# Queries and keys by crossbar transfer from the ninth step on in an attention and mixer kernel

## The chip, the cores and the metric

The kernel runs on one core of a Trainium2 chip. The metric is the device time of one execution in microseconds; the kernel before took 371.93 us (median of 3 runs, 371.04 to 372.26). A core has five engines with instruction streams of their own: TensorE (PE, with its weight loads as PEld), VectorE (DVE), ScalarE (ACT), GpSimd (POOL) and SyncE (SP). In this kernel GpSimd issues the loads from memory, and SyncE issues the transposing transfers and nearly all of the output stores.

## The reference

Attention with squared ReLU over 8 batches of 12 heads, 448 tokens and 64 dimensions, and then a mixer with a token part and a channel part:

```python
scores = scale * np.matmul(q, k.transpose(0, 1, 3, 2))       # 8 x 12 heads, 448 x 448
attn = np.maximum(scores, 0.0) ** 2 / S
attn_out = np.matmul(attn, v)                                # 448 x 64 per head
x = attn_out.transpose(0, 2, 1, 3).reshape(B, S, H * D)      # 8 x 448 x 768

xt = x.transpose(0, 2, 1)
h = np.maximum(xt @ w_tok1, 0.0) @ w_tok2                    # token part, 448 -> 256 -> 448
u = x + h.transpose(0, 2, 1)
h2 = np.maximum(u @ w_ch1, 0.0) @ w_ch2                      # channel part, 768 -> 1536 -> 768
return (u + h2)
```

## The kernel before

The work goes in 24 steps of four heads each (ND = 24, three steps to a batch, DB = 3). Steps are named by their index, so step 8 is the ninth. Inputs are loaded as bf16 with tokens on the partitions, while the scores need the head dimension there: queries and keys have to be transposed for each step. Up to step 11 TensorE does this through PSUM (`transposes`); from step 12 on (`TDMA = 12`) VectorE puts the four heads next to each other in one buffer, `qk_sb`, and one crossbar transfer on SyncE's queue writes the transposed tile (`transposes_dma`).

```python
TDMA = 12

def transposes(i, place="acc", split=False):          # on TensorE, by 64x64 blocks
    sb = attn.tile([128, 2, 2, S], BF16, name="qkT", bufs=3)
    ...                                               # two PSUM tiles, acc0 and acc1
    for w in (0, 1):                                  # queries, keys
        src = raws.pop((i, "qk"[w]))
        for c in range(QC):                           # 7
            for r in range(2):
                for g in range(2):
                    nc.tensor.matmul(parts[r][...], lhsT=src[h, g, c, :],
                                     rhs=ident[h, h], is_transpose=True, ...)
    for r in range(2):
        nc.vector.tensor_copy(sb[:, r]..., parts[r][:, : 2 * S])

def interleave(i):
    t = attn.tile([128, 2, QC, 2, D], BF16, name="qk_sb", bufs=1)
    qk_tiles[i] = t
    for w in range(2):
        nc.vector.tensor_copy(t[:, w].rearrange("n c g d -> n g c d"),
                              raws.pop((i, "qk"[w])))

def transposes_dma(i):
    sb = attn.tile([128, 2, QC, 128], BF16, tag="qkT", name="qkT_x", bufs=3)
    nc.sync.dma_start_transpose(out=sb..., in_=qk_tiles.pop(i)...)
    qkT[i] = sb
```

The attention output `xT` has to be turned back for the token part (`x_back`: on TensorE up to step 7, by crossbar from step 8 on), and so does the residual `uT` for the last sum of the channel part (`u_back`: two crossbar transfers for each step). `hold_back` lets GpSimd write one element into the target of the residual transposes, so that they start only after a chosen event. The loop from step 4 on, cut to the order of its parts:

```python
for i in range(DB + 1, ND + 2):
    scores(i, 0); scores(i, 1)
    values(i - 1, range(QC)); values_out(i - 1)       # writes xT
    scores(i, 2)
    if TDMA <= i + 2 < ND:
        interleave(i + 2)
    ...                                               # fill: units of channel1 or channel2
    x_back(i - 1)
    if i > 2 * DB + 1:
        if i == 2 * DB + 2:                           # step 8
            hold_back(1, x_tiles[i - 1][:1, 0, 0, :1])
        while u_later and u_later[0] < max(i - 1 - (i == 2 * DB + 2), 0):
            u_back(u_later.pop(0))
    if TDMA <= i + 2 < ND:
        transposes_dma(i + 2)
    if i + PRE < ND:                                  # PRE = 3
        if i - 1 >= XDMA:                             # XDMA = 8
            nc.gpsimd.tensor_copy(gate, x_tiles[i - 1][:1, 1, 3, 127:])
        load_four(i + PRE)
    if i == 5:
        load_wc2(1, 2); load_wt1_last()               # the last of the weights
    square()
    ...
    scores(i, 3); scores(i, 4)
    if i + 1 < min(ND, TDMA):
        transposes(i + 1)
    square()
    ...                                               # fill, then token1_main(i - 1)
    token1_rest(i - 1)                                # from step 7 on
    scores(i, 5); scores(i, 6)
    square()
    ...                                               # fill
    token2(i - 1)                                     # its sums write uT
    if (i - 1) % DB == DB - 1:
        channel_work((i - 1) // DB)
    if i == 2 * DB + 1:                               # step 7
        hold_back(0, uT_tiles[1][:1, 0, :1])
        for _ in range(DB):
            u_back(u_later.pop(0))
    square()
    ...                                               # fill
```

A unit of `channel2` is twelve matmuls into one PSUM tile of two (`bank`), which a sum on VectorE empties into `out_sb`, adding the transposed residual `u_sb`; a store on SyncE's queue follows for each finished row tile.

Of the kernel before, what the change touches and what calls it, by code (L numbers as in the profile page):

```python
# [16 lines left out]
def kernel(  # L17
# [19 lines left out]
    ND = B * H // 4  # L37
# [143 lines left out]
            else:  # L181
                nc.vector.tensor_copy(sb[:, :, 0], queries[:, :, :S])

    TDMA = 12
    qk_tiles = {}

    def interleave(i):
# [4 lines that stand above are left out]
            nc.vector.tensor_copy(  # L192
                t[:, w].rearrange("n c g d -> n g c d"), raws.pop((i, "qk"[w]))
            )

    def transposes_dma(i):
        sb = attn.tile([128, 2, QC, 128], BF16, tag="qkT", name="qkT_x", bufs=3)
        nc.sync.dma_start_transpose(
            out=sb.rearrange("n w c t -> n (w c) t"),
            in_=qk_tiles.pop(i).rearrange("n w c g d -> n (w c g d)"),  # L200
        )
        qkT[i] = sb

    def qk_of(i, h, r):
        sb = qkT[i]
        if i < TDMA:
            return sb[h, r, 0, :], [sb[h, r, 1, c * 64 : (c + 1) * 64] for c in range(QC)]
# [3 lines left out]
    def scores(i, c, alone=False):  # L211
        ps = ps_att.tile([128, 2, 512], FP32, tag="att", name="sc_ps")
        for r in range(2):
            for g in range(2):
                h = slice(64 * g, 64 * (g + 1))
                queries, keys = qk_of(i, h, r)
                nc.tensor.matmul(  # L217
                    ps[64 * r : 64 * (r + 1), g, :S],
                    lhsT=keys[c],
                    rhs=queries,  # L220
                    start=True,
                    stop=True,
                    skip_group_check=True,
                )
        at = attn.tile([128, 2, S], BF16, name="at", bufs=11)
        if alone:
            nc.vector.tensor_scalar(
                out=at, in0=ps[:, :, :S], scalar1=0.0, scalar2=None, op0=ALU.max
            )
        else:  # L230
            nc.scalar.activation(at, ps[:, :, :S], AF.Relu)  # L231
        squares.append(at)
        at2[i, c] = at

    def square(keep=0):
        while len(squares) > keep:
            at = squares.pop(0)
            nc.vector.tensor_tensor(out=at, in0=at, in1=at, op=ALU.mult)  # L238

    def values(i, cs):  # L240
        v_raw = raws[i, "v"]
        if i not in accs:
            accs[i] = [ps_acc.tile([128, 512], FP32, tag=f"acc{r}", name="acc_ps") for r in range(2)]
        ps = accs[i]
        for c in cs:
            at = at2.pop((i, c))
            for r in range(2):
                for g in range(2):
                    h = slice(64 * r, 64 * (r + 1))
                    nc.tensor.matmul(  # L250
                        ps[r][64 * g : 64 * (g + 1), :S],
                        lhsT=v_raw[h, g, c, :],
                        rhs=at[h, g, :],
                        start=(c == 0),
                        stop=(c == QC - 1),
                        skip_group_check=True,
                    )

    def values_out(i, split=False):
        b, d = divmod(i, DB)  # L260
        ps = accs.pop(i)
        for r in range(2):
            if split and r == 1:
                nc.scalar.activation(
                    xT[b % 2][:, 2 * d + r, :S], ps[r][:, :S], AF.Copy, scale=float(alpha2)
                )
                continue
            nc.vector.tensor_scalar(  # L268
                out=xT[b % 2][:, 2 * d + r, :S],
                in0=ps[r][:, :S],  # L270
                scalar1=float(alpha2),
                scalar2=None,
                op0=ALU.mult,
            )
        if i > 2 * DB - 1:
            for r in range(2):
                nc.vector.tensor_scalar(
                    out=xT[b % 2][:, 2 * d + r, S:],
                    in0=ps[r][:, S - 64 : S],
                    scalar1=float(alpha2),  # L280
                    scalar2=None,
                    op0=ALU.mult,
                )
# [119 lines left out]
    def chunks(b):  # L403
        half = NT // 2
        return range(half) if b % 2 == 0 else range(half, NT)
# [12 lines left out]
    def hold_back(b, src):  # L418

        u_tiles[b] = mix.tile([128, NP, NT - NT // 2, 128], BF16, name="u_sb", bufs=3)  # L420
        for p in range(NP):
            nc.gpsimd.tensor_copy(u_tiles[b][:1, p, 0, :1], src)

    def channel1(b, e):
        if b % 2 == 0 and e == 0 and b > 0:
            r2_tiles[b // 2] = mix.tile([128, EC, 2 * S], BF16, name="r2_sb")
        uT, r2 = uT_tiles[b // 2], r2_tiles[b // 2]
        off = (b % 2) * S
        ps = ps_mm.tile([128, 512], FP32, tag="bank", name="m1_ps")
        for g in range(CC):  # L430
            nc.tensor.matmul(  # L431
                ps[:, :S],
                lhsT=wc1[:, g, e * 128 : (e + 1) * 128],
                rhs=uT[:, g, off : off + S],
                start=(g == 0),
                stop=(g == CC - 1),
            )
        nc.scalar.activation(r2[:, e, off : off + S], ps[:, :S], AF.Relu)  # L438
# [87 lines left out]
    def channel_work(b):  # L526
        for e in range(2 if b == 0 else 0, EC):
            queue.append((C1, lambda e=e: channel1(b, e)))
        for t in chunks(b):
            for j in range(2):  # L530
                last = b == B - 1 and t == NT - 1 and j == 1
                unit = channel2_last if last else channel2
                args = (b, t) if last else (b, t, j)
                later.append((C2, lambda unit=unit, args=args: unit(*args)))
        if b > 0:
            queue.extend(later)
            later.clear()
# [91 lines left out]
    i = DB  # L629
# [31 lines left out]
    for i in range(DB + 1, ND + 2):  # L661
        slow = i <= 2 * DB
        back = i - 1 < ND
        if i == 2 * DB + 1:
            rate[0] = (EC * C1 + NT * C2) / DB
        if i < ND:
            scores(i, 0)
            scores(i, 1)
        if 0 <= i - 1 < ND:
            values(i - 1, range(QC))  # L670
            values_out(i - 1)
        if i < ND:
            scores(i, 2)
        if TDMA <= i + 2 < ND:
            interleave(i + 2)
        if i - 1 < XDMA:
            fill(1 / 3, least=1)
        if 0 <= i - 1 < ND:
            x_back(i - 1)
        since[0] = 0.0  # L680
        if i > 2 * DB + 1:
            if i == 2 * DB + 2:
                hold_back(1, x_tiles[i - 1][:1, 0, 0, :1])
            while u_later and u_later[0] < max(i - 1 - (i == 2 * DB + 2), 0):
                u_back(u_later.pop(0))
        if TDMA <= i + 2 < ND:
            transposes_dma(i + 2)
        if i + PRE < ND:
            if i - 1 >= XDMA:
# [3 lines that stand above are left out]
            load_wc2(1, 2)  # L693
            load_wt1_last()
        square()
        if i - 1 >= XDMA:
            fill(0.37, least=1)
        if i < ND:
            scores(i, 3)
            scores(i, 4)  # L700
# [3 lines that stand above are left out]
        if slow:  # L704
            token1(i - 1)
            fill(1 / 3, least=1)
        else:
            fill(0.37, least=1, upto=4400 if back else 0)
            if back:
                token1_main(i - 1)  # L710
        if i < ND:
            if not slow:
                token1_rest(i - 1)
            scores(i, 5)
            scores(i, 6)
        elif back:
            token1_rest(i - 1)
        if not slow:
            square()
            fill(0.1, least=1)  # L720
        if back:
            token2(i - 1)
            if (i - 1) % DB == DB - 1:
                channel_work((i - 1) // DB)
        if i == 2 * DB + 1:
            hold_back(0, uT_tiles[1][:1, 0, :1])
            for _ in range(DB):
                u_back(u_later.pop(0))
        square()
        fill(1 / 3 if slow else 0.16, least=1)  # L730
    while queue:
        queue.pop(0)[1]()
# [30 lines left out]
```

## Time and profile before

The profile is of one execution with a span of 369.8 us. A group is a line of the kernel on one engine; its columns are the number of instructions, the time that they were busy, and the mean of one.

| group | count | busy us | mean ns |
|---|---|---|---|
| TensorE, channel1, L431 | 564 | 115.7 | 353 |
| TensorE, channel2, L470 | 660 | 113.2 | 326 |
| TensorE, values, L250 | 672 | 40.7 | 351 |
| TensorE, scores, L217 | 336 + 336 | 27.5 + 25.7 | 360, 356 |
| VectorE, squares, L238 | 168 | 98.1 | 621 |
| VectorE, output sums, L477 | 55 | 30.5 | 555 |
| ScalarE, ReLU of the scores, L231 | 167 | 144.9 | 922 |

| transfers | count | median us to landing |
|---|---|---|
| queries, keys, values, loads from GpSimd | 48, 46, 48 | 4.7, 6.2, 6.5 |
| residual transposes, SyncE | 48 | 2.5 |
| x_back transposes, SyncE | 16 | 3.2 |
| output stores, SyncE | 54 | 3.1 |

TensorE's matmuls overlap in the records, so busy times of its groups can add up to more than the time that passed. "To landing" is the time from the issue on the queue until the transfer's completion was signalled. On the queue SP a row of the timeline gives the time that the queue spent with issuing, not the transfer. The crossbar transfers of queries and keys (12, steps 12 to 23) land 4.0 to 7.9 us after issue, median 6.1.

### The profile page before, as it was taken

The page shows a single profiled execution, that of the slowest core. Times are in us where ns is not written, and L with a number is a line of the kernel's source. Part 1 is how long each engine was busy: PE and PEld are TensorE (multiplying, and loading weights), DVE is VectorE, ACT ScalarE, POOL GpSimd, SP SyncE. Part 2 cuts the span into 40 slices and gives each one's busy share as a digit, 9 for nine tenths or more (in the row PEclk, how much of TensorE's full clock was granted, in tenths as well). Part 3 has the DMA queues.
Part 4 walks back from the last instruction along what each step waited for, and adds up shares of the span by engine and source line. Part 5 has one row for each costly group of instructions (what it writes and reads, how often), then busy time and mean ns, then how long its engine had stood idle before and what let it go on. Part 6 is the DMA issues. An engine that isn't in the chain of part 4 may idle for free.

```text
span 369.8 us, 8951 instructions
## 1 busy us (share of the span) xinstructions
PE 359.9 (97%) x3705; PEld 193.5 (52%) x3705; DVE 207.3 (56%) x414; ACT 210.5 (57%) x313; POOL 98.6 (27%) x185
## 2 busy tenths in 40 slices
PE   8889999999999999999999999999999999999995
PEld 3534555455555644555445545455445555555563
DVE  2986688756575774565654674575564674221031
ACT  4987888777245457735775457753875456402400
POOL 8957347303304404430421404412300000000000
PEclk9999999999999999999999999999999999999999
DMA  8999999932999899969768989759682624233023
GB/s 155 112 193 193 192 206 174 152 48 56 109 189 160 141 236 139 157 118 210 140 109 152 127 185 182 141 99 210 125 144 52 135 57 88 59 71 87 0 74 98
DMA packets 91449, 48.75 MB, mean 132 GB/s; under 512 B 65360, under 2 KB 87952, under 8 KB 91408
## 3 DMA queue, kind: packets, MB, share of 16 engines
q0 software_dynamic: 24496, 21.49, 41.0%
q1 hardware_dynamic: 66528, 26.26, 33.5%
q8 instruction: 29, 0.48, 0.5%
q10 hardware_dynamic: 384, 0.43, 0.4%
q14 instruction: 12, 0.10, 0.1%
HBM read 43.42 MB, written 11.01 MB: 147 GB/s over the span
## 4 chain that ended last, share of the span: by engine, by line
PE 86%; DVE 5%; DMA 4%; POOL 2%; issue 1%; ACT 1%; DVEq 0%; POOLq 0%; ACTq 0%
PE m_ps L431 28%; PE m_ps L470 28%; PE acc_ps L250 9%; PE sc_ps L217 8%; PE h_ps L380 4%; PE t_ps L339 3%; DVE at L238 1%; DMA x_sb<-xT 1%; PE t_ps L321 1%; DVE uT_sb L390 1%; DMA q_raw<-in_q_dram 1%; PE t_ps L355 1%; DMA k_raw<-in_k_dram 1%; PE qkT_ps L140 1%; POOL q_raw L83 1%
## 5 line engine op out<-in xcount | busy, mean ns | idle before, releaser
L231 ACT ACTIVATE at<-sc_ps 128x896 bf16<-128x896 f32 x167 | 144.9, 922 | 49.2 <-PE sc_ps L217 44.8
L238 DVE TENSOR_TENSOR at<-at 128x896 bf16<-128x896 bf16 x168 | 98.1, 621 | 59.9 <-ACT at L231 59.8
L431 PE MATMUL m_ps<-uT_sb,wc 128*128 128x448 bf16 x564 | 115.7, 353 | 0.4 <-DVE out_sb L477 0.2
L470 PE MATMUL m_ps<-wc,r_sb 128*128 128x384 bf16 x660 | 113.2, 326 | 0.0
L470 PEld LDWEIGHTS <-r_sb 128*128 128x128 bf16 x660 | 62.7, 98 | 47.9 <-issue 7.5
L438 ACT ACTIVATE r_sb<-m_ps 128x448 bf16<-128x448 f32 x94 | 51.5, 548 | 53.4 <-PE m_ps L431 53.4
L431 PEld LDWEIGHTS <-wc 128*128 128x128 bf16 x564 | 52.3, 98 | 56.3 <-issue 11.6
L477 DVE TENSOR_TENSOR out_sb<-m_ps,u_sb 128x384 f32<-128x384 f32 x55 | 30.5, 555 | 48.7 <-PE m_ps L470 45.5
L250 PE MATMUL acc_ps<-at,v_raw 64*64 64x448 bf16 x672 | 40.7, 351 | 1.6 <-DVE x_sb L312 0.8
L268 DVE TENSOR_SCALAR xT<-acc_ps 128x448 bf16<-128x448 f32 x45 | 26.1, 620 | 27.6 <-PE acc_ps L250 27.6
L690 POOL COPY gate<-x_sb 1x1 bf16<-1x1 bf16 x12 | 2.3, 196 | 122.5 <-DMA x_sb<-xT 122.5
L83 POOL DMA_DIRECT2D q_raw<-in_q_dram x48 | 29.0, 612 | 21.4 <-DMA wc<-in_moe_w_ch_dram 17.6
L390 DVE TENSOR_TENSOR uT_sb<-h_ps,xT 128x448 bf16<-128x448 f32 x48 | 27.7, 616 | 9.4 <-PE h_ps L380 9.3
L83 POOL DMA_DIRECT2D v_raw<-in_v_dram x48 | 29.4, 634 | 7.2 <-DMA wc<-in_moe_w_ch_dram 4.7
L250 PEld LDWEIGHTS <-v_raw 64*64 64x64 bf16 x672 | 21.4, 106 | 15.8 <-issue 5.8
L365 ACT ACTIVATE r_sb<-t_ps 128x256 bf16<-128x256 f32 x36 | 11.9, 381 | 30.5 <-PE t_ps L355 30.5
L83 POOL DMA_DIRECT2D k_raw<-in_k_dram x46 | 28.1, 626 | 2.0 <-issue 1.9
L217 PE MATMUL sc_ps<-qkT 64*64 64x448 bf16 x336 | 27.5, 360 | 1.0 <-ACT at L231 0.8
L217 PE MATMUL sc_ps<-qkT_x 64*64 64x448 bf16 x336 | 25.7, 356 | 0.0
L380 PE MATMUL h_ps<-wt,r_sb 128*128 128x448 bf16 x96 | 22.3, 353 | 0.0
L217 PEld LDWEIGHTS <-qkT 64*64 64x64 bf16 x336 | 9.2, 105 | 12.9 <-issue 10.5
L339 PE MATMUL t_ps<-x_sb,wt 128*128 128x256 bf16 x108 | 14.7, 273 | 0.1
(62 smaller groups left out, 162.1 us busy)
## 6 DMA issues: line engine op xcount, KB each, us to landing
out_dram<-out_sb SPq DMA_DIRECT2D x54, 192.0 KB, 3.1
q_raw<-in_q_dram POOLq DMA_DIRECT2D x48, 112.0 KB, 4.7
v_raw<-in_v_dram POOLq DMA_DIRECT2D x48, 112.0 KB, 6.5
k_raw<-in_k_dram POOLq DMA_DIRECT2D x46, 112.0 KB, 6.2
wc<-in_moe_w_ch_dram POOLq DMA_DIRECT2D x4, 1152.0 KB, 11.7
u_sb<-uT_sb SPq DMA_TRANSPOSE x48, 2.5
x_sb<-xT SPq DMA_TRANSPOSE x16, 3.2
k_first<-in_k_dram SPq DMA_DIRECT2D x1, 224.0 KB, 3.5
```

What stands on the lines that cost most here:

```text
L83: eng.dma_start(out=dst[64 * r : 64 * (r + 1)].rearrange("p g c d -> p g (c d)"), in_=src[b, h0 : h0 + 2].rearrange("g (p c) d -> p g (c d ...
L217: nc.tensor.matmul(ps[64 * r : 64 * (r + 1), g, :S], lhsT=keys[c], rhs=queries, start=True, stop=True, skip_group_check=True,)
L231: nc.scalar.activation(at, ps[:, :, :S], AF.Relu)
L238: nc.vector.tensor_tensor(out=at, in0=at, in1=at, op=ALU.mult)
L250: nc.tensor.matmul(ps[r][64 * g : 64 * (g + 1), :S], lhsT=v_raw[h, g, c, :], rhs=at[h, g, :], start=(c == 0), stop=(c == QC - 1), skip_gro ...
L268: nc.vector.tensor_scalar(out=xT[b % 2][:, 2 * d + r, :S], in0=ps[r][:, :S], scalar1=float(alpha2), scalar2=None, op0=ALU.mult,)
L380: nc.tensor.matmul(parts[r][:, :S], lhsT=r1[:, j, r * 128 : (r + 1) * 128], rhs=wt2[:, j, :], start=(j == 0), stop=(j == JC - 1),)
L390: nc.vector.tensor_tensor(out=uT_tiles[b // 2][:, 2 * d + r, off : off + S].rearrange("n (c p) -> n c p", c=QC), in0=parts[r][:, :S].rearr ...
L431: nc.tensor.matmul(ps[:, :S], lhsT=wc1[:, g, e * 128 : (e + 1) * 128], rhs=uT[:, g, off : off + S], start=(g == 0), stop=(g == CC - 1),)
L438: nc.scalar.activation(r2[:, e, off : off + S], ps[:, :S], AF.Relu)
L470: nc.tensor.matmul(ps[:, :HN], lhsT=r2[:, e, t * 128 : (t + 1) * 128], rhs=wc2[:, e, cols], start=(e == 0), stop=(e == EC - 1),)
L477: nc.vector.tensor_tensor(out=o[:, cols].rearrange("n (g d) -> n g d", d=128), in0=ps[:, :HN].rearrange("n (g d) -> n g d", d=128), in1=u_ ...
```

## The change

Queries and keys go by crossbar from step 8 on in place of step 12 on, so that TensorE is spared the 64x64 transposes of steps 8, 9, 10 and 11, and VectorE their copies out of PSUM. The place of the transfer in the loop is as before for step 9 and from step 11 on (in the middle of the step that lies two ahead of its use). For steps 8 and 10 it is put at the end of step 6 and of step 7. The three transfers of steps 8, 9 and 10 are thereby all issued between the last loads of weights (in step 5) and the first residual transposes (end of step 7). The call of `square()` at the end of a step moves ahead of the residual transposes.

```diff
-    TDMA = 12
+    TDMA = 8
...
-        if TDMA <= i + 2 < ND:
+        crossed = (TDMA + 1, *range(TDMA + 3, ND))
+        if i + 2 in crossed:
             interleave(i + 2)
...
-        if TDMA <= i + 2 < ND:
+        if i + 2 in crossed:
             transposes_dma(i + 2)
...
             if (i - 1) % DB == DB - 1:
                 channel_work((i - 1) // DB)
+        square()
+
+        if i in (TDMA - 2, TDMA - 1):
+            n = TDMA if i == TDMA - 2 else TDMA + 2
+            interleave(n)
+            transposes_dma(n)
         if i == 2 * DB + 1:
             hold_back(0, uT_tiles[1][:1, 0, :1])
             for _ in range(DB):
                 u_back(u_later.pop(0))
-        square()
         fill(1 / 3 if slow else 0.16, least=1)
```

## The prediction

> **What bounds the kernel now.** I read the page first (busy time by engine, the slices, the chain), then, for the steps that the change touches, the timeline of TensorE and of the transfer queue SP, the waits of VectorE, and the landing times of single transfers. Steps are named by the loop index: step 8 is the ninth. The first scores of a step mark its start on TensorE: step 6 near 59.9 us, step 7 at 69.5, step 8 at 84.4, step 9 at 101.7, step 10 at 117.0, step 11 at 132.1.
>
> ```profile
> PE 359.9 (97%) x3705; PEld 193.5 (52%) x3705; DVE 207.3 (56%) x414; ACT 210.5 (57%) x313; POOL 98.6 (27%) x185
> PE 86%; DVE 5%; DMA 4%; POOL 2%; issue 1%; ACT 1%; DVEq 0%; POOLq 0%; ACTq 0%
> ```
>
> TensorE is busy 97% of the span and makes up 86% of the chain that ended last. A matmul taken out is a gain only if nothing else then holds TensorE up. So the question is how much slack the other engines and the transfers have in steps 6 to 11. Three views answer it. The timeline of the queue SP:
>
> ```profile
> 84.80 18.26 SPq L413 DMA_TRANSPOSE u_sb<-uT_sb  x12
> 103.15 2.54 SPq L489 DMA_DIRECT2D out_dram<-out_sb  x4
> 105.79 1.65 SPq L294 DMA_TRANSPOSE x_sb<-xT  x1
> 107.50 6.00 SPq L413 DMA_TRANSPOSE u_sb<-uT_sb  x4
> ```
>
> SP does nothing until 84.80, then is occupied without a gap until 107.4: twelve residual transposes, four output stores, and then x_back of step 8, the first one that goes by crossbar. Its input was ready on VectorE at 105.07 (xT writes end there), so it was the queue that let it go at 105.79. The waits of VectorE in step 8 and the timeline at the end of this row:
>
> ```profile
> DVE out_sb L477 <- DMA u_sb<-uT_sb: 3.2, 1, 3.2
> 110.91 0.33 PEld L339 LDWEIGHTS <-wt 128*128 128x128 bf16 x4 [0.45 <-DMA x_sb<-xT]
> ```
>
> The first says that the second output sum of step 8 waited 3.2 us, until 97.76, for the sixth residual transpose. The second says that token1_main of step 8 began at 110.91 just as x_sb landed (105.79 + 5.1): TensorE waited some 0.23 us, as that stretch took 4.14 us from the start of the 24 matmuls before it, against 3.91 one step later. So in steps 8 and 9 **the queue SP is a second bound, with no slack**, although TensorE is shown as busy.
>
> **What the Trainium skill says.** "DMA: Bandwidth & Descriptors", section Anatomy of one DMA: a wait for a semaphore happens on the issuing sequencer, ahead of dispatch. So a transfer whose input is late holds back those behind it on SP; the trace agrees, since x_back left the queue 0.7 us after its input was ready. The same page, section Queues, rings and completion order: each DMA engine takes turns between the queues by packet, and within a ring keeps their order. The trace agrees: a residual transpose lands 2.3 to 2.5 us after issue with nothing beside it (84.8 to 89), and 7.8 and 8.6 us after it when the load of step 11 is in flight (issued 93.8 and 95.1). "TensorE: Matmul & The Clock Gate", section Part 4: PE-mode transpose, gives about 275 ns for one 128x128 transpose in a kernel; here the 64x64 ones have 193 ns each but run packed, 56 of them in 0.58 us, and I use the latter. "Advanced Engine Details and Errata", section X-Bar Transpose, calls these transfers as fast as ordinary ones; that would be, by an estimate from its 350 to 400 GB/s, 1.2 us for 128x14x128 of two bytes. The trace shows 4.0 to 7.9 us to landing, which I use.
>
> **The change part by part.** *Taken from TensorE:* the transposes of queries and keys for steps 8, 9, 10 and 11, which stand in steps 7, 8, 9 and 10.
>
> ```profile
> 89.97 0.39 PE L140 MATMUL qkT_ps<-ident,q_raw 64*64 64x64 bf16 x28
> 90.18 0.43 PE L140 MATMUL qkT_ps<-ident,k_raw 64*64 64x64 bf16 x28
> 90.55 1.31 PE L431 MATMUL m_ps<-uT_sb,wc 128*128 128x448 bf16 x6
> ```
>
> From 89.97 to 90.55 is 0.58 us; four such blocks are 4 x 0.58 = 2.3 us. All of it lies on the chain. That is the most that can be had: 371.93 - 2.3 = 369.6.
>
> *VectorE:* eight copies out of PSUM go (0.62 us each); eight copies into qk_sb come (0.39 us, two in 0.69 us). VectorE is at 56%, so only where the new copies stand in its order matters.
>
> *First new place, end of step 6.* The copy for step 8 follows the squares that end at 70.26 and ends at 70.95, in a gap that VectorE has anyway until 71.46. The transfer goes at 71.0, while the load of step 10 (issued from 70.46) is in flight. Beside loads this shape lands after 5.5 to 7.9 us: 76.5 to 78.9. It is needed at 83.9, in time. But qk_sb has one buffer, and the copy for step 9 now stands only half a step later (72.9, after xT), so VectorE is held there until the transfer has landed. With 78.0 it copies until 78.7, and x_sb of step 6 is copied by 79.4. TensorE would want that at 79.90 - 0.58 = 79.3. I put down **0.5 us** lost (0 to 1.0).
>
> *Second new place, end of step 7.* The copy for step 10 stands behind the two sums of token2, which ended at 85.06: now 85.06 - 0.58 + 0.5 = 84.98, and 85.67 after the copies. The transfer of step 10 is issued then and holds SP 1.54 us (the usual time of this shape), until 87.3. Only behind it come the twelve residual transposes, which had gone at 84.80, on a signal of the first of the two sums. They **start 2.5 us later**.
>
> *What that starts.* (a) The sixth is issued 6.67 us after the first: at 94.0 in place of 91.47. That moves it into the load of step 11 (from about 92), where 7.8 us to landing was seen: 101.8 in place of 97.76. The second output sum waits for it and ends at 102.4; the unit of channel2 that needs its PSUM bank began at 99.67 and could begin at 99.67 - 1.16 + 0.5 = 99.0, but now begins at 102.4, 2.7 us later than before. (b) SP is through with residuals and stores at 105.7 + 2.5 = 108.2; xT of step 8 is ready at 105.07 + 2.7 = 107.8. x_back goes at 108.3, lands 5.1 us later, and token1_main starts at 113.4 in place of 110.91: 2.5 us later. (a) and (b) come from one delay and don't add; the later one counts.
>
> *Steps 9 and 10.* The third and fourth blocks of transposes: the one in step 9 lies ahead of token1_main and is eaten by (b); the one in step 10 is gained, 0.58 us. There SP had been idle from 116.6 to 120.55, so the crossbar transfer of step 11 (1.5 to 2.6 us of SP) fits.
>
> Sum: +2.5 - 0.58 = +1.9 us; 371.93 + 1.9 = **373.9 us**.
>
> **The rivals.** *One: the transfers are hidden and the gain is whole, 369.6.* For it: TensorE's share of 97%, and SP idle until 84.8. The first two transfers do fall in that idle time. Against it: the third is issued by the same VectorE work that lets the residuals go, so it can't be ahead of them. *Two: residuals issued later meet less of the load, land faster and give some time back.* Against: twelve at about 1.5 us each are bound by the queue; for: x_back could land in 3.2 us, as in the later steps, once the load of step 11 is through, which makes (b) 1.9 us less. Then (a) counts alone, and the end would be near 373.0 to 373.5. *Three: VectorE, held by the single qk_sb, becomes the bound of step 7,* with the transfer of step 8 at 8 us or more, or the copies of step 9 waiting for their load as well (keys of step 9 landed at about 72.4, half a microsecond ahead). Each microsecond there is passed on to everything behind it: 374.5 to 376.
>
> **Range and chances.** The low end lets the chain be delayed only by the transfer itself (1.5 us), with no loss in step 7 and a fast x_back: some 371.4. The high end adds 1.0 us in step 7 and a landing of 9 us for the sixth residual: 376.2. Within 2% is 364.5 to 379.4, which holds all of the rivals. I give a small rest to a larger stall that I don't see.
>
> **What would show it.** Right: the group of 64x64 transposes falls from 616 to 392 matmuls (two inputs); a wait of VectorE on qkT_x of several microseconds near 73; residuals starting on SP at about 87; the wait of out_sb on u_sb grown beyond 3.2 us; TensorE idle in steps 8 and 9 by 3 to 4 us; x_sb to token1_main ending later than 110.9. Wrong: residuals that start before 86, or land well under 7 us; then the gain of rival one comes through. A wait elsewhere, in step 10 for the transfer of step 11 or on output stores, would be a step that I have left out.

## The result, and the profile after

The changed kernel takes 383.69 us (median of 4 runs, 382.62 to 384.39) against 372.1 us before (median of 4 runs): a ratio of 1.0313 with a 95% interval of 1.0279 to 1.0347. It is 11.6 us slower, where 1.9 us had been predicted.

The page of the kernel after, share of the chain that ended last, and two groups of TensorE (busy us, mean ns | idle time ahead of them and what ended most of it):

```profile
PE 76%; DMA 12%; DVE 6%; POOL 2%; ACT 2%; issue 1%; SPq 0%; DVEq 0%; ACTq 0%
...
L431 PE MATMUL m_ps<-uT_sb,wc 128*128 128x448 bf16 x564 | 117.9, 357 | 5.6 <-DVE x_sb L312 5.2
L470 PE MATMUL m_ps<-wc,r_sb 128*128 128x384 bf16 x660 | 115.0, 329 | 3.4 <-DVE out_sb L477 3.4
```

TensorE had 86% of the chain and has 76% now; transfers went from 4% to 12%. Two waits stand ahead of TensorE's matmuls that were not there: 5.2 us for x_sb and 3.4 us for out_sb. The same groups are also slower in themselves, by 2.2 and 1.8 us. The timeline of TensorE before, at these two places in steps 7 and 8 (start, us, ..., in brackets the idle time ahead, if any):

```profile
75.35 4.71 PE L431 MATMUL m_ps<-uT_sb,wc 128*128 128x448 bf16 x24
...
99.67 2.11 PE L470 MATMUL m_ps<-wc,r_sb 128*128 128x384 bf16 x12
```

And after:

```profile
75.74 1.31 PE L431 MATMUL m_ps<-uT_sb,wc 128*128 128x448 bf16 x6
82.28 5.57 PE L431 MATMUL m_ps<-uT_sb,wc 128*128 128x448 bf16 x18 [5.22 <-DVE x_sb L312]
...
106.23 0.92 PE L380 MATMUL h_ps<-wt,r_sb 128*128 128x448 bf16 x4
110.35 3.74 PE L470 MATMUL m_ps<-wc,r_sb 128*128 128x384 bf16 x12 [3.20 <-DVE out_sb L477]
```

What TensorE waited for in step 7 is a short copy on VectorE. VectorE's timeline after shows what stood ahead of it:

```profile
73.41 0.35 DVE L277 TENSOR_SCALAR xT<-acc_ps 128x64 bf16<-128x64 f32 x2
80.93 0.39 DVE L192 COPY qk_sb<-q_raw 128x896 bf16<-128x896 bf16 x1 [7.18 <-DMA qkT_x<-qk_sb]
81.24 0.39 DVE L192 COPY qk_sb<-k_raw 128x896 bf16<-128x896 bf16 x1
81.54 0.68 DVE L312 COPY x_sb<-x_ps 128x1024 bf16<-128x1024 bf16 x1
```

The first two lines of L192 are the copy for step 9. It waited 7.18 us for the transfer of step 8 to leave qk_sb (issued at 71.83, landed 9.0 us later). In step 8 the chain of residuals is the one that was predicted. The timeline of the queue SP after:

```profile
71.83 23.22 SPq L198 DMA_TRANSPOSE qkT_x<-qk_sb  x3
95.11 17.03 SPq L413 DMA_TRANSPOSE u_sb<-uT_sb  x12
112.23 3.59 SPq L489 DMA_DIRECT2D out_dram<-out_sb  x4
117.40 1.23 SPq L294 DMA_TRANSPOSE x_sb<-xT  x1
118.68 5.17 SPq L413 DMA_TRANSPOSE u_sb<-uT_sb  x4
```

And VectorE's timeline in step 8:

```profile
109.74 0.56 DVE L477 TENSOR_TENSOR out_sb<-m_ps,u_sb 128x384 f32<-128x384 f32 x1 [7.89 <-DMA u_sb<-uT_sb]
```

The sums of token2 on VectorE, at whose first one the residuals may start, before and then after:

```profile
83.91 1.15 DVE L390 TENSOR_TENSOR uT_sb<-h_ps,xT 128x448 bf16<-128x448 f32 x2
...
91.70 1.15 DVE L390 TENSOR_TENSOR uT_sb<-h_ps,xT 128x448 bf16<-128x448 f32 x2
```

The residuals leave 3.41 us after the start of the first sum (91.70 to 95.11) where it was 0.89 us (83.91 to 84.80); the second output sum waits 7.9 us in place of 3.2. The slower matmuls show in the stretches of the kernel after. Columns: stretch in us, its length, busy time of PE, PEld, DVE, ACT and POOL, then the granted clock, the DMA share and GB/s.

```profile
82.00:88.00 6.00, 5.72 (x21) 2.57 (x21) 2.90 (x6) 1.20 (x3) 0.00 (x0) 0.63 0.41 76
88.00:92.20 4.20, 4.20 (x37) 1.96 (x35) 1.67 (x3) 3.15 (x6) 0.00 (x0) 1.00 0.00 0
...
110.30:114.00 3.70, 3.65 (x12) 1.61 (x11) 2.60 (x5) 0.00 (x0) 0.00 (x0) 0.54 0.77 155
114.00:128.60 14.60, 14.60 (x131) 8.08 (x130) 9.53 (x20) 6.62 (x9) 3.98 (x7) 1.00 0.83 131
```

After each long wait TensorE has 0.63 and 0.54 of its clock for some microseconds, then 1.00 again. The length of each step, from its first scores on TensorE to those of the next, in the profiled executions:

| us | before | after | two qk_sb | ten on TensorE | only ten | eleven on TensorE |
|---|---|---|---|---|---|---|
| step 7 | 14.86 | 21.78 | 14.38 | 19.82 | 14.86 | 14.39 |
| step 8 | 17.32 | 21.84 | 22.47 | 16.84 | 22.11 | 16.85 |
| step 9 | 15.33 | 14.61 | 14.61 | 15.66 | 14.61 | 14.61 |
| step 10 | 15.09 | 14.99 | 14.61 | 19.82 | 15.09 | 15.08 |
| step 11 | 11.68 | 12.30 | 12.66 | 11.67 | 11.67 | 11.68 |

Steps 7 to 11 take 85.52 us after and 74.28 before, 11.2 us of the 11.6.

### The profile page after: what moved, and what is told of

The parts are those of the page before. It is cut to its first block, busy times and chain, and to the rows that moved or that the text cites. A ratio compares the mean times of both kernels' runs of the same rounds, so it can differ in the third digit from the quotient of the medians.

```text
span 382.2 us, 8519 instructions
## 1 busy us (share of the span) xinstructions
PE 362.2 (95%) x3481; PEld 191.9 (50%) x3481; DVE 206.1 (54%) x414; ACT 210.2 (55%) x313; POOL 100.1 (26%) x185
## 4 chain that ended last, share of the span: by engine, by line
PE 76%; DMA 12%; DVE 6%; POOL 2%; ACT 2%; issue 1%; SPq 0%; DVEq 0%; ACTq 0%
PE m_ps L470 25%; PE m_ps L431 24%; PE acc_ps L250 8%; PE sc_ps L217 7%; DMA qkT_x<-qk_sb 5%; PE h_ps L380 4%; PE t_ps L339 3%; DMA x_sb<-xT 2%; DVE at L238 2%; DMA u_sb<-uT_sb 2%; DMA v_raw<-in_v_dram 2%; PE t_ps L321 1%; DVE uT_sb L390 1%; DMA k_first<-in_k_dram 1%; PE t_ps L355 1%
## 5 line engine op out<-in xcount | busy, mean ns | idle before, releaser
L431 PE MATMUL m_ps<-uT_sb,wc 128*128 128x448 bf16 x564 | 117.9, 357 | 5.6 <-DVE x_sb L312 5.2
L470 PE MATMUL m_ps<-wc,r_sb 128*128 128x384 bf16 x660 | 115.0, 329 | 3.4 <-DVE out_sb L477 3.4
L431 PEld LDWEIGHTS <-wc 128*128 128x128 bf16 x564 | 52.8, 99 | 63.8 <-issue 20.3
L217 PE MATMUL sc_ps<-qkT_x 64*64 64x448 bf16 x448 | 34.1, 356 | 0.0
L217 PE MATMUL sc_ps<-qkT 64*64 64x448 bf16 x224 | 19.0, 362 | 1.1 <-ACT at L231 0.9
L217 PEld LDWEIGHTS <-qkT_x 64*64 64x64 bf16 x448 | 11.0, 105 | 11.7 <-issue 10.6
```

The lines of the kernel that those rows point to most:

```text
L217: nc.tensor.matmul(ps[64 * r : 64 * (r + 1), g, :S], lhsT=keys[c], rhs=queries, start=True, stop=True, skip_group_check=True,)
L431: nc.tensor.matmul(ps[:, :S], lhsT=wc1[:, g, e * 128 : (e + 1) * 128], rhs=uT[:, g, off : off + S], start=(g == 0), stop=(g == CC - 1),)
L470: nc.tensor.matmul(ps[:, :HN], lhsT=r2[:, e, t * 128 : (t + 1) * 128], rhs=wc2[:, e, cols], start=(e == 0), stop=(e == EC - 1),)
```

## The experiments

**Theory:** one buffer for qk_sb and one place in VectorE's order make step 7 wait; the third transfer ahead of the residuals makes step 8 wait; each wait is followed by a low clock. **Rivals:** the crossbar transfers cost by themselves wherever they stand; the slow matmuls come from contention. Each ratio is to runs of the kernel before taken together with the experiment, whose median was 371.25 to 371.44 us.

### Two buffers for qk_sb

```diff
-    k_first = consts.tile([128, 2, QC, D], FP32, name="k_first")
+    k_first = attn.tile([128, 2, QC, D], FP32, tag="qk_sb", name="k_first", bufs=2)
...
-        t = attn.tile([128, 2, QC, 2, D], BF16, name="qk_sb", bufs=1)
+        t = attn.tile([128, 2, QC, 2, D], BF16, name="qk_sb", bufs=2)
```

> The changed kernel with two buffers for qk_sb (the second lies where k_first was, which is free after step 0); the order of all instructions stays. My theory: in step 7 VectorE stood 7.2 us at the copy for step 9 because qk_sb has one buffer and the transfer of step 8 took 9.0 us to land; x_sb stood behind it, its PSUM tile is one of the two of the tag bank, and TensorE's second unit of channel1 needs that tile. Then the wait goes, TensorE's 5.2 us idle in step 7 go, and so does the low clock after it (2.0 us): about 376.5 us, with the 3.2 us idle of step 8 left. Rival (the crossbar transfers themselves are too much for the queues, whoever waits for them): the wait moves to another instruction of step 7 or 8 and the time stays at 382 to 384.

Measured: 376.69 us, ratio to before 1.0142 (1.0119 to 1.0165). TensorE's timeline in step 7 and step 8 of this kernel:

```profile
75.48 4.71 PE L431 MATMUL m_ps<-uT_sb,wc 128*128 128x448 bf16 x24
...
103.58 3.48 PE L470 MATMUL m_ps<-wc,r_sb 128*128 128x384 bf16 x12 [4.09 <-DVE out_sb L477]
```

The 24 matmuls of channel1 run without a gap and step 7 is 14.38 us long: the single buffer was the cause of that wait and of the low clock behind it, 7.4 us together. The wait of step 8 stays. All instructions stand in the same order, and the same transfers are made. In this profile the transfer of step 8 landed after 5.6 us in place of 9.0, but that is not why the wait is gone: in the last kernel below, also with two buffers, it landed after 9.9 us, and TensorE doesn't wait in step 7 either.

### The copy for step 9 behind that of x_sb

```diff
-        if i + 2 in crossed:
+        if i + 2 in crossed and i != 7:
             interleave(i + 2)
...
             x_back(i - 1)
+        if i == 7:
+            interleave(i + 2)
```

> The changed kernel with one buffer for qk_sb as it is, but the copy for step 9 stands behind that of x_sb on VectorE, not ahead of it. My theory: x_sb is copied at once, its PSUM tile comes free and TensorE goes on with channel1; VectorE still waits some 7 us at the copy for step 9, but what stands behind (squares) is needed only at the end of step 7. About 376.5 to 377.5 us. Rival (TensorE needs the squares or the sums behind the copy just as early): 381 or more.

Measured: 377.86 us, ratio 1.018 (1.0156 to 1.0204). VectorE's timeline in this kernel:

```profile
74.15 0.69 DVE L312 COPY x_sb<-x_ps 128x1024 bf16<-128x1024 bf16 x1 [1.59 <-PE x_ps L303]
80.40 0.39 DVE L192 COPY qk_sb<-q_raw 128x896 bf16<-128x896 bf16 x1 [5.56 <-DMA qkT_x<-qk_sb]
```

And TensorE's:

```profile
74.55 4.71 PE L431 MATMUL m_ps<-uT_sb,wc 128*128 128x448 bf16 x24
...
85.43 0.38 PE L250 MATMUL acc_ps<-at,v_raw 64*64 64x448 bf16 x2 [1.26 <-DVE uT_sb L390]
```

VectorE still waits 5.6 us at the same copy, but TensorE goes through channel1 without a gap. So it was not the transfer's result that TensorE missed, nor x_sb for token1_main (the matmuls that waited, L431, read uT_sb and wc), but the copy that empties x_ps: x_ps has one of the two PSUM tiles of the tag `bank`, and the second unit of channel1 needs it. What stays of the wait reaches TensorE later, 1.4 us at the sums of token2.

### Step 10 on TensorE

```diff
...
-        if i + 1 < min(ND, TDMA):
+        if i + 1 < min(ND, TDMA) or i + 1 == TDMA + 2:
             transposes(i + 1)
...
-        if i in (TDMA - 2, TDMA - 1):
-            n = TDMA if i == TDMA - 2 else TDMA + 2
+        if i == TDMA - 2:
+            n = TDMA
```

> The changed kernel with step 10 transposed on TensorE as before, so that no crossbar transfer stands between the sums of token2 and the residual transposes; steps 8, 9 and 11 stay with the crossbar. My theory: the residual transposes start about 0.9 us after the first sum of token2, as in the kernel before (now 3.4 us), the wait of out_sb falls from 7.9 to about 3 us, TensorE's idle time of 3.2 us in step 8 and the low clock after it (1.6 us) go, and 0.6 us for the transposes comes back: about 379.5 us. The 5.2 us of step 7 stay. Rival (the residuals are late because step 7 as a whole is late and they meet the load of step 11): 383 to 384.

Measured: 379.74 us, ratio 1.0226 (1.0175 to 1.0277). The timeline of SP in this kernel:

```profile
89.54 18.68 SPq L413 DMA_TRANSPOSE u_sb<-uT_sb  x12
```

And that of TensorE in steps 8 and 10:

```profile
103.94 2.11 PE L470 MATMUL m_ps<-wc,r_sb 128*128 128x384 bf16 x12
...
132.06 3.44 PE L470 MATMUL m_ps<-wc,r_sb 128*128 128x384 bf16 x12 [3.72 <-DVE out_sb L477]
```

The residuals start on time again (0.89 us after the first sum of token2, at 88.65), and step 8 is free of waits, 16.84 us long, as expected. The call of `square()` is moved in this kernel as in the change, so it is not what made them late. That the time fits so well is partly chance: in the profiled execution step 7 lost less than before (3.58 us idle, the transfer of step 8 landed after 7.3 us), while step 10 lost 3.72 us. There the copy for step 12 waited for the transfer of step 11, which took 11.0 us to land: the single buffer once more.

### Step 10 alone by crossbar

The kernel before with the transfer of step 10 at the end of step 7, as in the change, and nothing else moved to the crossbar:

```diff
-    TDMA = 12
+    TDMA = 8
...
-        if i < TDMA:
+        if i < 12 and i != 10:
...
-        if TDMA <= i + 2 < ND:
+        crossed = range(12, ND)
+        if i + 2 in crossed:
             interleave(i + 2)
...
-        if i + 1 < min(ND, TDMA):
+        if i + 1 < 12 and i + 1 != 10:
             transposes(i + 1)
...
+        square()
+
+        if i == TDMA - 1:
+            n = TDMA + 2
+            interleave(n)
+            transposes_dma(n)
         if i == 2 * DB + 1:
...
-        square()
```

> The kernel before with step 10 alone by crossbar, copy and transfer at the end of step 7 ahead of the residual transposes as in the changed kernel; steps 8, 9 and 11 stay on TensorE, so no copy into qk_sb waits for another transfer. My theory: the residual transposes start 2.5 us later, the sixth lands in the load of step 11, out_sb waits 7 us or more, TensorE is idle some 3 us in step 8 and then runs 12 matmuls at a lower clock (1.5 us); 0.6 us of transposes are saved: about 375.5 us. Rival (the delay of the residuals hurts only together with the lateness of step 7): 371 us.

Measured: 375.01 us, ratio 1.0093 (1.0062 to 1.0124). VectorE's timeline in step 8 of this kernel:

```profile
102.38 0.56 DVE L477 TENSOR_TENSOR out_sb<-m_ps,u_sb 128x384 f32<-128x384 f32 x1 [7.08 <-DMA u_sb<-uT_sb]
```

And TensorE's:

```profile
102.99 3.78 PE L470 MATMUL m_ps<-wc,r_sb 128*128 128x384 bf16 x12 [2.95 <-DVE out_sb L477]
```

One transfer at this place costs 4.8 us in step 8, by the table, with no other part of the change present but the moved call of `square()`.

### Zero matmuls in the waits

```diff
+    def spin(pool, tag, shape, n):
+        ps = pool.tile(shape, FP32, tag=tag, name="spin_ps")
+        dst = ps if len(shape) == 2 else ps[:, 0, :]
+        for _ in range(n):
+            nc.tensor.matmul(dst, lhsT=warm[:, :128], rhs=warm, start=True, stop=True)
...
+            if i == 7:
+                idle_hook.append(lambda: spin(ps_acc, "acc0", [128, 512], 22))
             fill(0.37, least=1, upto=4400 if back else 0)
...
+        if i == 8:
+            spin(ps_att, "att", [128, 2, 512], 14)
         fill(1 / 3 if slow else 0.16, least=1)
```

The tile `warm` holds zeros; `idle_hook` runs after the first unit of channel1 in this fill.

> The changed kernel with idle matmuls of zeros where TensorE stood: 22 of 128x512 in step 7 ahead of the second unit of channel1, 14 in step 8 ahead of the last unit; their results are used by nothing, and nothing is left out. They take no more time than the waits. My theory: after each wait TensorE ran at a granted clock of 0.63 and 0.54 for some microseconds, which cost 2.0 us (18 matmuls in 5.57 us in place of 3.58) and 1.6 us (12 in 3.74 us in place of 2.11). Without the idle time the clock stays at 1.0 and the time falls by about 3.6 us to 380.1, though the waits stay. Rival (the slow matmuls come from contention, not from the idle time): no less than 383.

Measured: 379.2 us, ratio 1.0218 (1.0163 to 1.0272); the granted clock over the whole execution is 1.000, against 0.987 in the kernel after. TensorE's timeline in this kernel:

```profile
75.52 4.91 PE L551 MATMUL spin_ps<-warm 128*128 128x512 bf16 x22
81.17 3.56 PE L431 MATMUL m_ps<-uT_sb,wc 128*128 128x448 bf16 x18 [0.74 <-DVE x_sb L312]
...
103.86 3.19 PE L551 MATMUL spin_ps<-warm 128*128 128x512 bf16 x14
106.89 2.11 PE L470 MATMUL m_ps<-wc,r_sb 128*128 128x384 bf16 x12
...
132.70 2.11 PE L470 MATMUL m_ps<-wc,r_sb 128*128 128x384 bf16 x12 [2.46 <-DVE out_sb L477]
```

More work on TensorE, and less time: the 18 and 12 matmuls behind the waits take 3.56 and 2.11 us in place of 5.57 and 3.74, though VectorE waits 7.4 us at qk_sb as in the kernel after. Steps 7 and 8 together take 39.9 us in place of 43.6, and 3.6 had been expected. The low clock comes from the idle time. The last line is a wait in step 10 that was not filled.

### All of steps 8 to 11 at the usual place, with one and with two buffers

The kernel before with `TDMA = 8`; in the second kernel also the diff of two buffers above.

> The kernel before with TDMA = 8 in place of 12 and nothing else: steps 8 to 11 go by crossbar too, each at the usual place in the middle of the step two ahead of its use, one buffer for qk_sb, the transfer of step 10 behind the twelve residual transposes. My theory: what costs in the changed kernel is where the transfers of steps 8 and 10 stand, not that they exist. Here a full step lies between two copies into qk_sb, so VectorE waits at most about 1.5 us in step 7 (the transfer of step 8 goes while weights are loaded and may land late), and the residuals start on time; only x_back of step 8 leaves SP some 1.6 us later. Sum: -2.3 us of transposes, +1.2 us of x_back beyond what it waits anyway, up to 1.5 us in step 7: 371 to 373 us. Rival (crossbar transfers of queries and keys in this part of the kernel cost by themselves, wherever they stand): 378 or more.

Measured: 381.05 us, ratio 1.0265 (1.0239 to 1.0291). My expectation missed. The transfer of step 8 in this kernel (issue on SP in ns; then us to landing):

```profile
L198 SPq DMA_TRANSPOSE qkT_x<-qk_sb x1: 6887/6887/6887, 63.9 to 63.9; - x1
...
DMA to landing us min/median/max: 14.9/14.9/14.9
```

Among the loads of weights it took 14.9 us, longer than the step between two copies, and VectorE waited 5.9 us for it. The number was the rival's, so the buffer was tried by itself:

> The kernel before with TDMA = 8 and two buffers for qk_sb (the second where k_first was), the places of all transfers as usual. With one buffer it took 381.05 us, against my 371 to 373: TensorE stood idle for 3.9, 2.8 and 1.9 us in steps 7, 8 and 10, each time behind a copy into qk_sb that waited for a transfer (the one of step 8, among the loads of weights, took 15 us to land), with low clock after the first two. My theory: the single buffer is the cause there too, and the transfers by themselves cost little: 370 to 372.5 us. Rival (so many crossbar transfers in this part cost by themselves): 377 or more.

(The second of the three idle times named there, 2.8 us, is in step 9, not 8.) Measured: 374.35 us (median of 22 runs, 371.67 to 379.67), ratio 1.006 (1.0041 to 1.0079); the two longest runs count as slow and are not in the ratio. The single buffer had cost 6.7 us here as well, by the medians, but the time is above what I expected and below the rival's. In step 7 TensorE still waits 0.98 us for x_sb, which stands behind the copies for step 9, and these waited 1.56 and 1.08 us for their loads. Most of what is left stands ahead of token1_main in step 9, on TensorE's timeline of the kernel with two buffers:

```profile
112.91 0.82 PE L339 MATMUL t_ps<-x_sb,wt 128*128 128x256 bf16 x6 [2.51 <-DMA x_sb<-xT]
...
114.27 3.81 PE L470 MATMUL m_ps<-wc,r_sb 128*128 128x384 bf16 x12
```

That is x_back of step 8, behind twelve residuals, the transfer of step 10 and the stores on SP; a low clock follows, not at once but 1.4 us after the wait (12 matmuls in 3.81 us). So transfers on this queue do cost by their place, even with two buffers. This speaks for the change's aim of having the third one ahead of the residuals, if it can be had early enough.

### Repairs

With two buffers, step 10 was put back on TensorE (both diffs above), or its copy and transfer were set ahead of the squares of the last two scores of step 7:

```diff
             token1_rest(i - 1)
+        if i == TDMA - 1:
+            interleave(TDMA + 2)
+            transposes_dma(TDMA + 2)
         if not slow:
             square()
...
-        if i in (TDMA - 2, TDMA - 1):
-            n = TDMA if i == TDMA - 2 else TDMA + 2
+        if i == TDMA - 2:
+            n = TDMA
```

> Both repairs together: two buffers for qk_sb, and step 10 on TensorE; steps 8, 9 and 11 go by crossbar, step 8 at the end of step 6. My theory: both waits of TensorE, in steps 7 and 8, and the low clock behind them are gone; three blocks of transposes (1.7 us) are saved, of which the one in step 8 is lost again to x_back of step 8, which the queue SP lets go too late: about 1.2 us faster than the kernel before, 370.2 us. If something else holds the transfers up, it shows as a time above 372.

Measured: 370.37 us, ratio 0.9968 (0.9954 to 0.9982). The time is as expected, the reason only in part: steps 8 and 9 are 16.85 and 15.09 us long, against 17.32 and 15.33 before, so the block in step 8 was not lost to x_back; but step 11 is 12.10 us long, against 11.68.

> Two buffers for qk_sb, and all of steps 8 to 11 by crossbar, but copy and transfer of step 10 stand some 3 us earlier than in the changed kernel: ahead of the squares of the last two scores of step 7, so ahead of the sums of token2. My theory: SP is then through with this transfer about when the residual transposes become ready, so they start within 1 us of their time in the kernel before, and out_sb waits little more than 3 us. The saved transposes of steps 8 and 9 are lost to x_back of step 8 on SP: about 370.3 us, as with step 10 on TensorE. Rival (the transfer of step 10 holds the residuals up on the rings even when it is issued earlier): TensorE still waits 2 us or more in step 8, 373 or more.

Measured: 371.26 us, ratio 0.9994 (0.9979 to 1.0009). Neither kernel waits in steps 7 and 8. In the second, steps 7, 8 and 9 are 14.39, 16.84 and 14.61 us long, so the transposes of steps 8 and 9 were not lost to x_back, against my expectation; but in step 10 TensorE waited 0.85 us for x_back of step 9.

> As the kernel with step 10 earlier, and the four output stores of step 8 are issued by GpSimd, which has nothing else to do then, in place of SP. They no longer stand ahead of x_back of step 8 on SP. My theory: in the kernel before, SP is the second bound of steps 8 and 9; without the stores x_back goes 1 to 2.6 us earlier and all four blocks of transposes (2.3 us) are gained: about 369.3 us. Rival (x_back is bound by landing, not by its place on the queue): no difference from the kernel with step 10 earlier.

Measured: 370.81 us, ratio 0.999 (0.9974 to 1.0007), not to be told from the kernel without it, as the rival said. The stores were not what held anything up by then.

> Two buffers for qk_sb, steps 8, 9 and 10 by crossbar with the transfer of step 10 ahead of the sums of token2, step 11 on TensorE. In the kernel with step 10 earlier, steps 7, 8 and 9 were 0.5, 0.5 and 0.7 us shorter than in the kernel before, but step 10 was 0.5 us longer, as x_back of step 9 landed 0.9 us too late behind the transfer of step 11. My theory: with step 11 on TensorE the three gains stay: about 1.6 us faster than the kernel before, 369.7 us. Rival (x_back lands late because of the loads, not the transfer): no more than 0.5 us faster than before.

Here `crossed` starts at step 12 apart from step 9, and `transposes` does step 11. Measured: 369.34 us, ratio 0.9938 (0.9922 to 0.9954): as expected, and 0.6% faster than the kernel before. The interval lies below that of the kernel with step 10 earlier, and meets that of the kernel with step 10 on TensorE. The timeline of SP in this kernel:

```profile
71.22 12.28 SPq L198 DMA_TRANSPOSE qkT_x<-qk_sb  x3
84.58 17.84 SPq L413 DMA_TRANSPOSE u_sb<-uT_sb  x12
```

The three transfers are off the queue at 83.5, ahead of the residuals, which start at 84.58; TensorE has no wait longer than 0.2 us in steps 6 to 11.

## Why the prediction was wrong

The direction and the place in step 8 were right, the sum was not: +1.9 us predicted, +11.6 measured. By its own steps:

- **Taken from TensorE, 4 x 0.58 = 2.3 us: too much.** Steps 7, 8 and 9 without the block and without waits are 0.48, 0.47 and, against step 10 before, 0.48 us shorter; four blocks are 1.9 us. The next unit starts 0.50 us after the scores where no block stands between (75.24 to 75.74 after), and the block itself had started 0.40 us after them (74.36 to 74.77 before); so of the 0.58 us from the start of the block to the next unit 0.48 are spared.
- **First new place, 0.5 us (0 to 1.0): this is the step that failed.** The wait of VectorE at the single qk_sb was foreseen. But I looked for the need of x_sb only at token1_main (79.3). The experiment with the copy behind x_sb shows that its PSUM tile is needed at once by the second unit of channel1, near 77 on the timeline after. TensorE stood 5.22 us in place of 0.5, 7.2 us with the low clock behind it. The landing was off too (9.0 us, where 7.0 was taken), but that is the lesser part: in the kernel with step 10 on TensorE the transfer landed after 7.3 us, and TensorE stood 3.58 us all the same. Rival three came nearest, with VectorE as the bound of step 7, but its 374.5 to 376 us add only 0.6 to 2.1 us to the sum.
- **The clock: left out of the prediction.** 2.0 us after the wait of step 7 and 1.6 us after that of step 8, shown by the zero matmuls. I had weighed every wait at its own length. "TensorE: Matmul & The Clock Gate", section Why this matters for your kernels, does warn of gaps above about 3 us; in the kernel after both waits, 5.22 and 3.20 us, were longer, and in the experiments 2.84 and 2.95 us brought a low clock too.
- **Second new place, residuals 2.5 us later: right.** Measured 3.41 - 0.89 = 2.52 us.
- **(a) The sixth residual: right.** Issued 7.6 us after the first (6.67 predicted), landed after 6.9 us (7.8); TensorE idle 3.2 us where 102.4 - 99.0 = 3.4 was predicted. The experiment with step 10 alone gives 2.95 us. That the load of step 11 is what slows its landing was not tested by itself.
- **(b) x_back of step 8: didn't come.** (a) had delayed xT as well, and x_back left SP as soon as xT was ready, at 117.40. (Here one sees a late input hold the queue: SP had been free from 115.82, and four residuals of which the last sums had ended at 112.9 left only behind x_back, at 118.68. The 0.7 us that the prediction gives for this show only a queue that was occupied.) Where the transfer of step 10 stood behind the residuals, in the kernel with the usual places and two buffers, it did come, with 2.51 us.
- **Step 11 fits on SP: right for the queue, wrong for the buffer.** TensorE waited only 0.23 us in step 10 of the profiled execution of the change, but 3.72, 2.46 and 1.94 us in three of the experiments with one buffer.

The waits and clocks add up: 5.22 + 2.0 + 3.20 + 1.6 + 0.23, and 0.6 us in step 11, less 1.9, make 11.0 us of the 11.2 that steps 7 to 11 grew by. Without the low clock steps 8 and 9 together grew by 2.2 us, close to the 2.5 us that the sum has for them. That is partly luck: the sum took them from (b), which did not come. The rest was not looked into, nor why the same transfer lands after 5.6 us in one kernel and 9.5 in another beside the same load.

## What to carry to other kernels

When a copy is moved up in an in-order engine, list everything that stands behind it and who holds a buffer of which there are only two; the first to need one sets the cost, not the obvious consumer. The same transfer took 4.0 us to land with no load beside it, up to 11.0 us beside the load of a step and 14.9 and 16.1 us among the loads of weights, so a single staging buffer needs the longest landing, not the median, between two uses. Price a wait of TensorE of 2.5 us or more at its length plus some 1.3 to 2.0 us of low clock, which is what the ten waits listed below cost.

## What the hardware showed that I had not expected

- The granted clock fell to 0.50 to 0.70 over the next 3.4 to 6 us after waits of 2.51, 2.84, 2.95, 3.20, 3.58, 3.72, 3.90, 4.09, 4.46 and 5.22 us, in seven of the kernels, and stayed at 1.00 after 1.94 and 2.46 us in two. After 2.51 us it stayed at 1.00 for another 1.4 us first. Whether a fixed length decides this is not shown, as the waits near 2.5 us were seen once each. In the kernel with matmuls of zeros in the waits the clock stayed at 1.00.
- A crossbar transfer of 128x14x128 held SP 1.5 us and landed after 4.0 us with no load beside it (steps 9 and 10 of the kernel after), but held SP 6.9 us and landed after 14.9 us among the loads of weights.
